# A planner's new numbers, filter-row DMAs behind the last root, and a last slab shared with GpSimd

## Chip, cores, metric

One core of one Trainium2 chip. The metric is the time of one execution in microseconds of device time (us). One core alone has no second die to compare with, so a run counts as slow when it is over 1.5% above the fastest of its kernel. Verdicts use fast runs alone and call 2% a difference; each kernel was timed in five rounds beside the kernel before on the same chip, and the ratios are read with their intervals.

## The reference

```python
def reference(A_x, A_w_r, A_w_i, B_x, B_w_gate, B_w_up, B_w_down):
    x  = A_x                                   # 1 x 2048 x 640, bf16
    xn = _layernorm(x)                         # over the 640 columns, eps 1e-5
    X  = rfft2(xn) * (A_w_r + 1j * A_w_i)      # spectral filter, 2048 x 321
    s  = irfft2(X)
    g  = silu((gelu(xn @ B_w_gate) * (xn @ B_w_up)) @ B_w_down)   # 640 -> 1536 -> 640
    return x + s * g
```

The kernel does both Fourier transforms by matmuls. The 2048 rows are 16 slabs of 128.

## The kernel before

Every instruction is a task with a cost. A planner in Python, run on the host while the program is built, simulates the engines and a model of the DMA bus, and the order in which it starts the tasks becomes the order of each engine's instructions. On the chip each engine runs its list in that order. So a number in the planner costs no instruction; it can only reorder them.

```python
    def ready(self, t, e, now):                     # earliest start of task t on engine e
        ...
        at = max([0.0] + [... a.done + (... self.MARGIN[e]
                 + ((1500 if a.size else 150) if e == "PE" and a.start > 20000 else 0)) for a in t.after])
        ...
        if t.size and e == "SP":                    # a DMA: not further ahead of the bus than BACKLOG = 3500 ns
            at = max(at, self.wire - self.BACKLOG)
    def run(self):
            ...
            if t.land:                              # the first loads: landing times typed in from a measurement
                self.wire = max(self.wire, t.land - 1000)
                t.done = t.land
            elif t.size:                            # every other DMA: the model of the bus
                self.wire = max(self.wire, now + occ + 900) + t.size * t.slow / 340.0
                t.done = self.wire + (... 2600 if now < 21000 else 1000) + t.lag
```

**Roots**: GpSimd computes 1/sqrt(variance) of each slab (L430, L431), and VectorE applies it (L445). **Fold**: four VectorE operations (L511, L514, L520, L525) fold two slabs for the first transform; TensorE multiplies (L538, L539), ScalarE copies the product out of PSUM into `mc` (L297; two buffers), and the sync queue stores it (`D<-mc`).

**Filter rows**: twelve small DMAs on GpSimd that put single rows of the filter in place. After them GpSimd loads slabs of x again for the residual (`xr`, 160 KB each, three buffers).

```python
            turned_w[0].append(add(lambda e, ...: nc.gpsimd.dma_start(out=D4[a:a + n, b, ri, 0:width], in_=rows(w, first, n, width)),
                                   "POOL", (600, 600), (9, ri, b, a), after=[roots[3]], size=5152))
```

## Time and profile before

| | before |
|---|---|
| time, median of 6 runs | 204.5 us (204.39 to 204.67) |
| span of the profiled run | 202.4 us, granted clock 0.996 |
| TensorE busy | 195.9 us, 97% |
| its only wait in mid-kernel | 0.5 us at 25 us (0.65 from start to start) |
| last matmul ends / last output issued | 197.86 / 199.47 us |

TensorE is busy from the first to the last microsecond of its list, so the time is the sum of its work, plus what it stops, plus the end after its last matmul. The lines are in the prediction. In the views, PE is TensorE, DVE VectorE, ACT ScalarE, POOL GpSimd, SP the sync queue; a timeline line has start, duration, engine, source line, operation, and in brackets how long the engine was idle before it and what ended that.

### The profile page before, as it was taken

The numbers are of one execution on the slowest core, as the hardware profiler recorded it, in microseconds if no ns is written. First come the engines' busy times: TensorE is split into PE (matmuls) and PEld (weight loads), VectorE is DVE, ScalarE is ACT, GpSimd is POOL, SyncE is SP. The second block draws the span as 40 slices with busy tenths as digits, with TensorE's granted clock in tenths as the row PEclk, the third lists the DMA queues.
The fourth block names the chain that finished last, engine by engine and source line by source line (L and its number), as shares of the span: only waits on it lengthen the run. The fifth ranks groups of instructions, "written<-read, shape, count | busy, mean of one in ns | idle before, by whom it ended". The sixth has DMA issues, their size and how long they took to land.

```text
span 202.4 us, 4147 instructions
## 1 busy us (share of the span) xinstructions
PE 195.9 (97%) x1546; PEld 118.2 (58%) x1546; DVE 147.9 (73%) x317; ACT 127.6 (63%) x227; POOL 33.4 (16%) x70
## 2 busy tenths in 40 slices
PE   7999999999999999999999999999999999999991
PEld 2994344677544555677754555567755554557780
DVE  3587889999422239899999898963226887778783
ACT  4989789975632566768776756533286656775521
POOL 2495454590000000000000000000000222111200
PEclk9999999999999999999999999999999999999998
DMA  6999999598859776313342111105900433344422
GB/s 175 327 320 340 352 390 221 122 171 292 272 176 371 221 198 130 102 59 89 117 130 74 60 65 65 68 0 156 416 14 0 120 88 102 108 110 130 133 97 66
DMA packets 35398, 32.62 MB, mean 161 GB/s; under 512 B 10798, under 2 KB 32306, under 8 KB 35378
## 3 DMA queue, kind: packets, MB, share of 16 engines
q1 hardware_dynamic: 33938, 29.49, 48.9%
q0 software_dynamic: 1152, 2.66, 5.1%
q10 hardware_dynamic: 288, 0.20, 0.6%
q8 instruction: 12, 0.20, 0.4%
q14 instruction: 8, 0.07, 0.1%
HBM read 22.51 MB, written 9.19 MB: 157 GB/s over the span
## 4 chain that ended last, share of the span: by engine, by line
PE 95%; DMA 1%; DVE 1%; issue 0%; ACT 0%; DVEq 0%
PE pg L891 26%; PE pu L891 25%; PE pg L968 13%; PE pu L968 13%; PE sp L703 3%; PE sp L836 3%; PE sp L778 2%; PE sp L812 2%; PE sp L538 2%; PE sp L676 2%; DMA X<-in_A_x_dram 1%; PE sp L696 1%; PE sp L830 1%; PE sp L461 1%; PE sp L484 1%; PE sp L659 0%
## 5 line engine op out<-in xcount | busy, mean ns | idle before, releaser
L891 PE MATMUL pg<-xnT,Wg 128*128 128x512 bf16 (+1 forms) x245 | 57.5, 366 | 0.0
L891 PE MATMUL pu<-xnT,Wu 128*128 128x512 bf16 (+1 forms) x245 | 57.5, 366 | 0.0
L908 DVE TENSOR_TENSOR uT<-pu,ge 128x512 bf16<-128x512 f32 x46 | 31.7, 689 | 25.3 <-PE pu L891 24.8
L904 ACT ACTIVATE ge<-pg 128x512 bf16<-128x512 f32 x46 | 27.7, 601 | 32.2 <-PE pg L891 32.1
L968 PEld LDWEIGHTS <-uT 128*128 128x128 bf16 x396 | 37.8, 98 | 13.6
L891 PEld LDWEIGHTS <-Wg 128*128 128x128 bf16 x285 | 25.4, 99 | 23.1
L891 PEld LDWEIGHTS <-Wu 128*128 128x128 bf16 x285 | 25.0, 98 | 21.2
L932 POOL DMA_DIRECT2D xr<-in_A_x_dram x16 | 8.9, 560 | 140.1 <-DVE res L956 140.1
L968 PE MATMUL pg<-Wd,uT 128*128 128x320 bf16 (+2 forms) x204 | 30.2, 293 | 0.0
L968 PE MATMUL pu<-Wd,uT 128*128 128x320 bf16 (+1 forms) x192 | 29.8, 297 | 0.0
L297 ACT CAST ma<-sp 128x644 bf16<-128x644 f32 (+1 forms) x32 | 23.4, 793 | 6.3 <-PE sp L703 3.3
L977 ACT ACTIVATE th<-pg 128x320 f32<-128x320 f32 (+2 forms) x17 | 7.3, 427 | 9.5 <-PE pg L968 8.7
L297 ACT CAST Vt<-sp 128x640 bf16<-128x640 f32 x16 | 10.8, 691 | 3.7 <-PE sp L812 3.7
L297 ACT CAST IU<-sp 128x640 bf16<-128x640 f32 x16 | 10.7, 693 | 3.0 <-PE sp L778 3.0
L982 DVE SCALAR_TENSOR_TENSOR G<-th,pu 128x320 bf16<-128x320 f32 (+1 forms) x16 | 7.7, 481 | 6.3 <-ACT th L977 6.2
L982 DVE SCALAR_TENSOR_TENSOR G<-th,pg 128x320 bf16<-128x320 f32 (+1 forms) x16 | 7.7, 479 | 6.2 <-ACT th L977 6.1
L977 ACT ACTIVATE th<-pu 128x320 f32<-128x320 f32 (+1 forms) x16 | 7.0, 440 | 7.4 <-PE pu L968 7.3
L297 ACT CAST mc<-sp 128x640 bf16<-128x640 f32 x16 | 10.8, 700 | 1.2 <-PE sp L539 1.2
L297 ACT CAST Z<-sp 128x1024 bf16<-128x1024 f32 x8 | 7.9, 1015 | 1.8 <-PE sp L676 1.7
L431 POOL TENSOR_TENSOR RSTD<-MVA,mh 128x1 f32<-128x1 f32 x12 | 8.1, 678 | 2.0 <-DVE MVA L413 1.2
L416 ACT ACTIVATE th<-X 128x640 bf16<-128x640 bf16 x11 | 8.1, 738 | 0.2
L756 DVE TENSOR_TENSOR R<-Y 64x644 bf16<-64x644 bf16 x16 | 7.8, 490 | 0.4
(109 smaller groups left out, 242.5 us busy)
## 6 DMA issues: line engine op xcount, KB each, us to landing
BU<-D SPq DMA_DIRECT2D x8, 640.0 KB
D<-mc SPq DMA_DIRECT2D x8, 320.0 KB
xr<-in_A_x_dram POOLq DMA_DIRECT2D x16, 160.0 KB, 3.5
D<-IU SPq DMA_DIRECT2D x8, 320.0 KB
out_dram<-res SPq DMA_DIRECT2D x15, 160.0 KB
Wg<-in_B_w_gate_dram SPq DMA_DIRECT2D x6, 320.0 KB
Wu<-in_B_w_up_dram SPq DMA_DIRECT2D x6, 320.0 KB
WF<-D SPq DMA_DIRECT2D x8, 161.0 KB
```

The lines of the kernel that those rows point to most:

```text
L297: return nc.scalar.copy(out=out, in_=in_) if e == "ACT" else nc.vector.tensor_copy(out=out, in_=in_)
L416: nc.scalar.activation(out=place(junk, (D,)), in_=x, func=ACT.Copy, scale=-1.0 / D, accum_out=less)
L431: nc.gpsimd.tensor_tensor(out=rstd, in0=var, in1=mh, op=ALU.pow)
L703: nc.tensor.matmul(into(q, ri), lhsT=sZ.tile[:, q, ri, :], rhs=FM[:, kinds[q][2] + (4 if ri and kind == 0 else 0), :], start=False, stop=T ...
L756: nc.vector.tensor_tensor(out=o, in0=Yf[:, ::-3, :], in1=Yf[:, 1:3, :], op=ALU.subtract)
L891: nc.tensor.matmul(ps.tile[:, lo:hi], lhsT=w[:, c, t * P:(t + 1) * P], rhs=XR[:, c, lo:hi] if early else xnT[:, c, grp * 512 + lo:grp * 51 ...
L904: nc.scalar.activation(out=ge.tile, in_=pg.tile if src is None else src, func=ACT.Gelu_apprx_tanh)
L908: nc.vector.tensor_tensor(out=u.tile, in0=pu.tile if src is None else src, in1=ge.tile, op=ALU.mult)
L932: nc.gpsimd.dma_start(out=sx.tile, in_=xv[:, n1, :])
L968: nc.tensor.matmul(ps.tile[:, 0:hi - lo], lhsT=uT[grp, ks[i]].tile[:, j * P:(j + 1) * P], rhs=Wd[:, ks[i], lo:hi], start=(i == 0), stop=(i ...
L977: nc.scalar.activation(out=th.tile[:, 0:hi - lo], in_=ps.tile[:, 0:hi - lo], func=ACT.Tanh, scale=0.5)
L982: nc.vector.scalar_tensor_tensor(out=G2.tile[:, lo:hi], in0=th.tile[:, 0:hi - lo], scalar=1.0, in1=ps.tile[:, 0:hi - lo], op0=ALU.add, op1 ...
```

## The change

The intent: take the filter-row DMAs out of GpSimd's way while it computes roots, take two operations out of VectorE's closing chain, and give the planner numbers that were thought to be nearer to the chip. One more warm-up matmul (dummy work at the start, `keep_warm`) comes with it. The diff is shortened; `...` marks cuts, and the comments are mine.

```diff
- ... (1500 if a.size else 150) if e == "PE" and a.start > 20000 ...
+ ... (1500 if a.size else 250) if e == "PE" and a.start > 20000 ...      # larger margin for TensorE
-                self.wire = max(self.wire, t.land - 1000)
+                self.wire = max(self.wire, t.land - 3200)                # the bus model
-    t = warmed = keep_warm(5, [t])
+    t = warmed = keep_warm(6, [t])
-            ss = [... (0, 4, k, t) if k else (1, -1, k, t) ...]           # rank of the column sums ...
+            ss = [... (0, 4, k, t) ...]
-            sums_out[k] = add(... (0, 9) ...)                             # ... and of their copy
+            sums_out[k] = add(... (0, -1) ...)
-                out=D4[...], in_=rows(...)), "POOL", (600, 600), ..., after=[roots[3]], size=5152))
+                out=D4[...], in_=rows(...)), "POOL", (600, 600), ..., after=[roots[15]], size=5152))
-  t = add(ends, "PE", c_pe(480, 320, 161, 161, 161, 161), ...)            # likewise 480 -> 530 in the inverse
+  t = add(ends, "PE", c_pe(550, 320, 161, 161, 161, 161), ...)            # dearer row-tile visits
-                nc.vector.tensor_tensor(out=yg...)                        # and res, in finish()
+                (nc.gpsimd if last and lo == 0 else nc.vector).tensor_tensor(out=yg...)
```

The larger bus number means: the planner takes the bus for free 3.2 us, not 1.0 us, before each typed-in landing time.

More of the change, by code (lines that the diff above doesn't have):

```diff
@@ L143, in ready @@
                 return None
-        at = max([0.0] + [a.start + a.engs[e][0] if a.on == e == "PE" else a.done + (0 if a.on == e and not a.size else self.MARGIN[e] + ((1500 if a.size else 150) if e == "PE" and a.start > 20000 else 0)) for a in t.after])
+        at = max([0.0] + [a.start + a.engs[e][0] if a.on == e == "PE" else a.done + (0 if a.on == e and not a.size else self.MARGIN[e] + ((1500 if a.size else 250) if e == "PE" and a.start > 20000 else 0)) for a in t.after])
         more = {}
@@ L472, in sums @@
                     nc.tensor.matmul(pt.tile[:, 1, 256 + t:257 + t], lhsT=w[:, c, t * P:t * P + P], rhs=ones, start=(c == 0), stop=(c == 4), skip_group_check=True)
-            ss = [add(lambda e, t=t: sums(e, t), "PE", (132, 370), (0, 4, k, t) if k else (1, -1, k, t), after=[got[t], raw[n1]], use=[pt]) for t in range(2)]
-            sums_out[k] = add(lambda e: copy_on(e, WSUM[:, 2 * k:2 * k + 2], pt.tile[:, 1, 256:258]), {"ACT": c_act(2), "DVE": c_dve(2, 1, True)}, None, (0, 9), after=ss, use=[pt])
+            ss = [add(lambda e, t=t: sums(e, t), "PE", (132, 370), (0, 4, k, t), after=[got[t], raw[n1]], use=[pt]) for t in range(2)]
+            sums_out[k] = add(lambda e: copy_on(e, WSUM[:, 2 * k:2 * k + 2], pt.tile[:, 1, 256:258]), {"ACT": c_act(2), "DVE": c_dve(2, 1, True)}, None, (0, -1), after=ss, use=[pt])
     for n1 in range(4):
@@ L610 @@
             turned_w[0].append(add(lambda e, ri=ri, w=w, a=a, n=n, b=b, first=first, width=width: nc.gpsimd.dma_start(
-                out=D4[a:a + n, b, ri, 0:width], in_=rows(w, first, n, width)), "POOL", (600, 600), (9, ri, b, a), after=[roots[3]], size=5152))
+                out=D4[a:a + n, b, ri, 0:width], in_=rows(w, first, n, width)), "POOL", (600, 600), (9, ri, b, a), after=[roots[15]], size=5152))
         turned_w[0].append(add(lambda e, ri=ri, w=w: nc.gpsimd.dma_start(out=D4[15:16, 1, ri, L:LP], in_=w[0:1, 0:1]), "POOL", (600, 600),
-                            (9, ri, 2), after=[roots[3]], size=64))
+                            (9, ri, 2), after=[roots[15]], size=64))
     def fetch(G):
@@ L713, in spectral @@
             if kind == 0:
-                t = add(ends, "PE", c_pe(480, 320, 161, 161, 161, 161), (0, 102 + 4 * G), new=[*pes, sE], use=[sz, sZ],
+                t = add(ends, "PE", c_pe(550, 320, 161, 161, 161, 161), (0, 102 + 4 * G), new=[*pes, sE], use=[sz, sZ],
                         after=[z_done, zt_done, tab_in["fm"], tab_in["ft"]])
@@ L842, in inverse @@
             if k == 0:
-                t = add(ends, "PE", c_pe(480, 320, 160, 160, 160, 160), (0, 299 + 4 * j), after=v_done + [tab_in["im"], tab_in["it"]],
+                t = add(ends, "PE", c_pe(530, 320, 160, 160, 160, 160), (0, 299 + 4 * j), after=v_done + [tab_in["im"], tab_in["it"]],
                         new=[*pys, y4], use=svs)
@@ L950, in f1 @@
                     place(yg, (D,))
-                nc.vector.tensor_tensor(out=yg.tile[:, lo:hi], in0=y.tile[:, n1 % 2, lo:hi], in1=G2.tile[:, lo:hi], op=ALU.mult)
+                (nc.gpsimd if last and lo == 0 else nc.vector).tensor_tensor(out=yg.tile[:, lo:hi], in0=y.tile[:, n1 % 2, lo:hi], in1=G2.tile[:, lo:hi], op=ALU.mult)
             def f2(e):
@@ L955, in f2 @@
                     place(res, (D,))
-                nc.vector.tensor_tensor(out=res.tile[:, lo:hi], in0=yg.tile[:, lo:hi], in1=sx.tile[:, lo:hi], op=ALU.add)
-            t = add(f1, "DVE", c_dve(hi - lo), rank, after=[y_done[n1]] + done, new=[yg] if first else [], use=[y, G2] if first else [y, G2, yg])
-            t = add(f2, "DVE", c_dve(hi - lo), rank, after=[t, xr], new=[res] if first else [], use=[yg, sx] if first else [yg, sx, res])
+                (nc.gpsimd if last and lo == 0 else nc.vector).tensor_tensor(out=res.tile[:, lo:hi], in0=yg.tile[:, lo:hi], in1=sx.tile[:, lo:hi], op=ALU.add)
+            slow = last and lo == 0
+            t = add(f1, *(("POOL", (700, 800)) if slow else ("DVE", c_dve(hi - lo))), rank, after=[y_done[n1]] + done, new=[yg] if first else [], use=[y, G2] if first else [y, G2, yg])
+            t = add(f2, *(("POOL", (700, 800)) if slow else ("DVE", c_dve(hi - lo))), rank, after=[t, xr], new=[res] if first else [], use=[yg, sx] if first else [yg, sx, res])
             dma(lambda: outv[:, n1, lo:hi], lambda: res.tile[:, lo:hi], (0, 0, n1), 256 * (hi - lo), after=[t], use=[res])
```

## The prediction

> **What bounds the kernel now.** I read the page first, then TensorE's waits, then the timeline where TensorE waited, then the timeline of the end. From the page, busy time and the chain that ended last:
>
> ```profile
> PE 195.9 (97%) x1546; PEld 118.2 (58%) x1546; DVE 147.9 (73%) x317; ACT 127.6 (63%) x227; POOL 33.4 (16%) x70
> ...
> PE 95%; DMA 1%; DVE 1%; issue 0%; ACT 0%; DVEq 0%
> ```
>
> TensorE is busy for 195.9 of 202.4 us and is 95% of the chain. Its waits, complete:
>
> ```profile
> PE sp L369 <- DVE uT L362: 1.2, 1, 1.2
> PE sp L538 <- DVE mb L525: 0.5, 1, 0.5
> PE sp L461 <- DMA X<-in_A_x_dram: 0.2, 1, 0.2
> ```
>
> Of the 6.5 us in which TensorE is not busy, 1.2 precede its first matmul, 0.5 are one wait in mid-kernel, 0.2 are for the first slab of x, and the remaining 4.5 are the stretch after its last matmul (197.03 + 0.83 = 197.86 us, to the end at 202.4). Busy is not full rate, so I checked it: the chain shows five 512-column matmuls of L891 in 1.08 us over and over, that is 216 ns each. Nothing in the middle can be sped up by reordering.
>
> The one wait in mid-kernel, from the timeline around it (start, duration, engine, line, idle before):
>
> ```profile
> 18.30 0.52 POOL L610 DMA_DIRECT2D D<-in_A_w_i_dram  x1 [0.71 <-DMA D<-in_A_w_r_dram]
> 18.90 0.18 POOL L430 TENSOR_SCALAR MVA<-MVA 128x1 f32<-128x1 f32 x1
> 19.16 0.57 POOL L431 TENSOR_TENSOR RSTD<-MVA,mh 128x1 f32<-128x1 f32 x1
> 19.69 0.61 POOL L610 DMA_DIRECT2D D<-in_A_w_i_dram  x1
> 20.33 0.58 POOL L431 TENSOR_TENSOR RSTD<-MVA,mh 128x1 f32<-128x1 f32 x1
> 20.94 0.45 DVE L445 TENSOR_SCALAR s<-X,MVA,RSTD 128x640 bf16<-128x640 bf16 x1 [1.86 <-POOL RSTD L431]
> 24.85 0.48 DVE L525 TENSOR_TENSOR mb<-ma 128x640 bf16<-128x640 bf16 x1
> 25.39 0.39 PE L538 MATMUL sp<-mb,F1T 128*128 128x512 bf16 x1 [0.49 <-DVE mb L525]
> ```
>
> This is a chain through GpSimd. Vector had the variance of slab 4 ready at 17.47 + 0.15 = 17.62 us (L413 in the timeline). Its root on GpSimd started at 20.33, 2.7 us late, because GpSimd was issuing filter-row DMAs and waiting for earlier ones to land. Vector stood idle for 1.86 us, so the fold of slabs 4 and 5 ended at 25.33 and TensorE waited for it.
>
> The end, after TensorE's last matmul:
>
> ```profile
> 198.21 0.29 DVE L986 TENSOR_TENSOR mc<-s,pg 128x128 f32<-128x128 bf16 x1
> 198.42 0.28 DVE L956 TENSOR_TENSOR res<-yg,xr 128x256 bf16<-128x256 bf16 x1
> 198.62 0.28 DVE L951 TENSOR_TENSOR yg<-s,G 128x256 bf16<-128x256 bf16 x1
> 198.73 0.94 SPq L304 DMA_DIRECT2D out_dram<-res  x2
> 198.82 0.28 DVE L989 SCALAR_TENSOR_TENSOR yg<-th,mc 128x128 bf16<-128x128 f32 x1
> 199.02 0.28 DVE L956 TENSOR_TENSOR res<-yg,xr 128x256 bf16<-128x256 bf16 x1
> 199.22 0.21 DVE L996 TENSOR_TENSOR res<-yg,xr 128x128 bf16<-128x128 bf16 x1
> 199.47 0.35 ACTq L998 DMA_DIRECT2D out_dram<-res  x1
> ```
>
> Here Vector is the bound: one small operation every 0.20 us. The last output is issued by 199.82 and the span ends 2.6 us later.
>
> **What the Trainium skill says.** "TensorE: Matmul & The Clock Gate", Part 1, gives start-to-start 426.7 ns cold and 215.7 ns warm for 512 columns. The trace agrees: 216 ns warm, and the weight loads of the warm-up matmuls stand 0.42 us apart (1.62, 2.04, 2.47 us in the timeline). "GPSIMD Engine Reference", section 3.1, puts two-input elementwise work at about 2.6 cycles of 1.2 GHz per element, and section 1 says that GpSimd shares its SBUF interfaces with VectorE, with contention from Vector instructions that have two SBUF inputs. The trace of before has no wide two-input operation on GpSimd, but it shows the contention: L430 on 128x1 takes 0.19 us at 33.11, and 1.57 us at 38.99, under a row of two-input Vector operations. "DMA: Bandwidth & Descriptors", on SWDGE (Anatomy of one DMA), gives a fixed cost near 2 us; here the twelve filter-row DMAs need 5.2 to 6.3 us from issue to landing, the xr loads 3.5 us, so the measured values are used.
>
> **The change part by part.** The diff touches four things, and the built order of instructions shows what becomes of them.
>
> 1. Filter-row DMAs after the last root. All twelve now stand behind the last root on GpSimd. The root of slab 4 can start at about 17.7 instead of 20.33. Vector's apply (L445) no longer waits 1.86 us, so the fold should end about 2 us earlier, near 23.4. TensorE meets that fold later in its own order: one more L891 group of five (1.08 us) precedes it. Reach in the new kernel without stalls: 25.39 - 0.49 - 0.17 (an uncertain part of the same pause: start-to-start it cost 0.66 beyond the matmul) + 1.08 = about 25.8, over 2 us after the fold. The pause goes. Gain 0.5 to 0.65 us, all on the path, since TensorE has no idle time after it.
>
> The DMAs themselves move to about 43 us (last root before: 42.97 + 0.55). Twelve issues of about 0.56 us are 6.7 us, plus about 2 us of waits for the queue's earlier landings (2.0 us before): issued by about 52, landed by about 58 at 6 us each. The first reader is the load of the filter tile at 63.41. Margin 5 us; cost 0. The xr loads behind them are needed from 158 us on.
>
> 2. The new numbers for the planner. The same matmuls are planned; counted by kind, the two orders differ by one warm-up matmul and nothing else. The row-tile groups (L696, L830: 16 visits) stay 16, each still costing about 0.1 us on entry and on leaving; calling them dearer changes only the order. Gain 0 directly.
>
> 3. Sixth warm-up matmul. It costs 0.43 us cold. The five end near 3.34 and the first slab of x is there at 3.71, so it fills the 0.18 us and overruns to 1.21 + 6 x 0.427 = 3.77: 0.06 late. The second slab lands for 5.33 after two more cold matmuls, which absorbs that. Cost 0 to 0.06. The ten one-column sum matmuls (L472) now precede the first ten L891 matmuls. These run cold until 6.25 us (0.11 instead of 0.056 us), so up to 4 x 0.055 = 0.2 us may be saved; but the roots of slabs 1 to 3 now come in another order, and the apply of slab 3 may be met early. I count 0.
>
> 4. GpSimd finishes columns 0 to 255 of the last slab. Vector loses two operations of 0.28 us; one (L956 at 198.42) is in the closing chain, so the last Vector operation comes 0.20 us earlier. Against it: 256 x 2.6 / 1.2 = 0.55 us (estimate by the skill's page) plus a fixed part of 0.2 (from L430's 0.19) to 0.5 is 0.75 to 1.05 us for each of two. They start near 196.8, where a 640-wide two-input Vector operation (0.48 us) is in the way, and the second meets the closing chain of two-input operations from 198.4 on. So GpSimd ends between 198.5 and 199.5. In the sync queue its output stands ahead of Vector's, which was ready for issue near 199.3 before. If GpSimd ends after about 198.9 it starts to delay both. Net: -0.2 to +0.4, counted as 0.
>
> Sum: -0.6 (part 1) + 0 + 0 + 0 = 204.49 - 0.6 = 203.9 us.
>
> **The rivals.**
> - New waits replace the old one. The whole order after 6 us is reshuffled, some 300 groups on TensorE, and an in-order engine stalls where the plan was too hopeful. For: the fold of slabs 6 and 7 now has two more Vector operations (L511, L908: about 1.0 us) ahead of its L525, which started at 39.03 before; it is met at about 40.95. Against: Vector gains the 1.9 us, so it should be done by 39.5; and the planner's margin for TensorE's waits grew by 0.1 us. Later, Vector is 95% busy from 80 to 120 us; the first spectral result R ended near 85.1 and TensorE used it at 86.4 before, and the new order leaves about the same. Two or three waits of 0.2 to 0.4 us would give 204.4 to 204.8.
> - GpSimd becomes the end of the kernel, as in part 4: 204.2 to 204.6.
> - The filter tile comes late, because the DMAs on GpSimd crawl under Vector's load. Then the sync queue stands behind one wait and everything for the spectral stage shifts: 206 or more. The 5 us of margin speak against it.
> - All goes well: the pause gone, 0.2 from the cold start, 0.2 at the end: 203.4.
>
> **Range and chances.** Three runs lie within 0.11 us, so noise is small. The gain is capped by what TensorE idles: even everything together is about 1 us (0.5%). Losses are limited only by new stalls. Predicted 203.9, range 203.2 to 204.7. Faster by over 2% would need 4.1 us out of the 6.5 idle ones: 1%. Slower by over 2% needs the late filter tile: 2%. Within 2%: 97%.
>
> **What would show it.** Right: no wait of TensorE for mb L525; GpSimd's root for slab 4 near 17.7 us and Vector's L445 without the 1.86 us; TensorE's last matmul ending near 197.3; the filter DMAs issued from 43 to 52 us, and the filter tile's load no later than before (63.41). Wrong: new lines among TensorE's waits; a gap at the filter load; GpSimd's two operations ending after 199 us with the sync queue waiting for GpSimd at the end.

## More of the kernel before

**RB**: the first two gate and up tiles are multiplied from raw x, before its statistics are known, and repaired on VectorE by a row tile that a DMA (`RB<-D`, after `D<-th`) spreads over the partitions:

```python
            m = add(... nc.vector.scalar_tensor_tensor(in0=RB[:, 1], ...), "DVE", ..., after=[out, rb_in, sums_out[k]])   # L921
            normed.append(add(... nc.vector.tensor_tensor(in1=RB[:, 0], op=ALU.mult), "DVE", ..., after=[m]))            # L923
```

## The result and the profile after

| | before | after |
|---|---|---|
| time, median of 6 runs | 204.5 us | 204.59 us (204.35 to 205.19) |
| TensorE busy | 195.9 us | 195.7 us |
| pause of TensorE at 25 us | 0.65 us | none |
| stops of TensorE from 26 to 55 us, start to start | none | 0.20 + 0.18 + 0.41 us |
| last matmul ends | 197.86 us | 198.00 us |
| from there to the issue of the last output | 1.61 us | 1.41 us |

The ratio of after to before is 1.0009, 95% interval 0.9994 to 1.0025. Ratios here are the mean time of one kernel's fast runs over that of the other's of the same rounds, so not quite the ratio of the medians. So the gain of 0.6 us that I predicted was not there, although the time lies in my range.

TensorE's waits after (us in total, times, longest):

```profile
PE sp L369 <- DVE uT L362: 1.2, 1, 1.2
PE sp L461 <- DMA X<-in_A_x_dram: 0.5, 1, 0.5
PE pu L891 <- DMA Wu<-in_B_w_up_dram: 0.3, 1, 0.3
PE sp L538 <- ACT mc L297: 0.2, 1, 0.2
```

The wait for `mb L525` is gone, as predicted; a small new one, for a copy by ScalarE, stands in its place. The view of waits shows less than is lost: a stop costs TensorE more from start to start than the idle that the view counts.

The timeline after, from the moved root to the new stops:

```profile
17.47 0.55 POOL L431 TENSOR_TENSOR RSTD<-MVA,mh 128x1 f32<-128x1 f32 x1 [0.68 <-DVE MVA L413]
...
23.46 0.48 DVE L525 TENSOR_TENSOR mb<-ma 128x640 bf16<-128x640 bf16 x1
...
28.89 0.69 ACT L297 CAST mc<-sp 128x640 bf16<-128x640 f32 x1 [1.85 <-DMA D<-mc]
...
30.09 0.75 DVE L921 SCALAR_TENSOR_TENSOR IU<-RB,WSUM,IU 128x512 f32<-128x512 f32 x1 [1.68 <-DMA RB<-D]
...
37.09 0.97 PE L969 MATMUL pu<-Wd,uT 128*128 128x320 bf16 x6
...
43.92 0.38 PE L538 MATMUL sp<-mb,F1T 128*128 128x512 bf16 x1 [0.24 <-ACT mc L297]
```

The first two lines are what I promised: the root starts when the variance is there, and the fold ends at 23.94 us instead of 25.33. The next two are new. ScalarE waits 1.85 us for a buffer whose store has not landed, and VectorE 1.68 us for the row tile RB. Before, neither waited; this is the first L921 in the timeline of before:

```profile
31.58 0.74 DVE L921 SCALAR_TENSOR_TENSOR IU<-RB,WSUM,IU 128x512 f32<-128x512 f32 x1
```

Then come the stops.

The page agrees: part 4 of the page (the chain that ended last) was 95% TensorE and 1% DMA before, and is now

```profile
PE 79%; DMA 10%; DVE 5%; SPq 2%; issue 1%; ACT 1%; DVEq 0%; ACTq 0%
```

and the chain in order of time has as its longest piece of that stretch

```profile
22.70 7.37 DMA RB<-D
```

Start and duration: the row tile left the queue at 22.70 us and landed at 30.07. I had the planner print its own dates while the program was built (arithmetic on the host, not a time of the chip): it expected RB at 30.20 us in the kernel before and at 28.18 us in the changed one. The chip did not follow the new number.

The end went as hoped. From the timeline after:

```profile
196.98 0.85 POOL L951 TENSOR_TENSOR yg<-s,G 128x256 bf16<-128x256 bf16 x1 [4.34 <-DVE G L983]
...
197.91 0.67 POOL L956 TENSOR_TENSOR res<-yg,xr 128x256 bf16<-128x256 bf16 x1
...
199.41 0.35 ACTq L999 DMA_DIRECT2D out_dram<-res  x1
```

GpSimd is done at 198.58 us, before VectorE, and the last output follows the last matmul 0.20 us sooner. So the trace has -0.65 (pause), +0.79 (new stops), -0.20 (end); the start came out even. The sum is -0.06 us, next to the measured 0.0 of the two spans.

### The profile page after: what moved, and what is told of

It reads as the page before. It is cut to its first block, busy times and chain, and to the rows that moved or that the text cites. A ratio compares the mean times of both kernels' runs of the same rounds, so it can differ in the third digit from the quotient of the medians.

```text
span 202.4 us, 4151 instructions
## 1 busy us (share of the span) xinstructions
PE 195.7 (97%) x1547; PEld 117.8 (58%) x1547; DVE 146.8 (73%) x314; ACT 127.2 (63%) x228; POOL 32.0 (16%) x72
## 4 chain that ended last, share of the span: by engine, by line
PE 79%; DMA 10%; DVE 5%; SPq 2%; issue 1%; ACT 1%; DVEq 0%; ACTq 0%
PE pu L891 20%; PE pg L891 20%; PE pg L969 11%; PE pu L969 11%; DMA RB<-D 4%; DMA D<-th 3%; PE sp L703 3%; PE sp L836 3%; DMA Wu<-in_B_w_up_dram 2%; PE sp L778 2%; PE sp L812 2%; PE sp L676 2%; SPq L502 1%; DMA D<-in_A_w_r_dram 1%; PE sp L696 1%; PE sp L830 1%
## 5 line engine op out<-in xcount | busy, mean ns | idle before, releaser
L969 PEld LDWEIGHTS <-uT 128*128 128x128 bf16 x396 | 37.7, 98 | 14.2 <-DVE uT L908 0.3
L891 PEld LDWEIGHTS <-Wg 128*128 128x128 bf16 x285 | 25.2, 98 | 23.4
L969 PE MATMUL pg<-Wd,uT 128*128 128x320 bf16 (+2 forms) x204 | 30.5, 293 | 0.0
L969 PE MATMUL pu<-Wd,uT 128*128 128x320 bf16 (+1 forms) x192 | 29.5, 297 | 0.0
L297 ACT CAST ma<-sp 128x644 bf16<-128x644 f32 (+1 forms) x32 | 23.4, 793 | 7.4 <-PE sp L703 3.4
L756 DVE TENSOR_TENSOR R<-Y 64x644 bf16<-64x644 bf16 x16 | 7.8, 490 | 0.4
L758 DVE TENSOR_TENSOR R<-Y 64x644 bf16<-64x644 bf16 x16 | 7.8, 486 | 0.3
```

The source lines that it names most:

```text
L297: return nc.scalar.copy(out=out, in_=in_) if e == "ACT" else nc.vector.tensor_copy(out=out, in_=in_)
L756: nc.vector.tensor_tensor(out=o, in0=Yf[:, ::-3, :], in1=Yf[:, 1:3, :], op=ALU.subtract)
L758: nc.vector.tensor_tensor(out=o, in0=Y[:, 0], in1=Y[:, 1], op=ALU.add)
L891: nc.tensor.matmul(ps.tile[:, lo:hi], lhsT=w[:, c, t * P:(t + 1) * P], rhs=XR[:, c, lo:hi] if early else xnT[:, c, grp * 512 + lo:grp * 51 ...
L969: nc.tensor.matmul(ps.tile[:, 0:hi - lo], lhsT=uT[grp, ks[i]].tile[:, j * P:(j + 1) * P], rhs=Wd[:, ks[i], lo:hi], start=(i == 0), stop=(i ...
```

## The experiments

All kernels gave correct results. "Frozen" means that the planned order of a kernel is kept and single tasks are moved in it; otherwise the planner ran again. The runs of before are from the same chip and rounds: one set of eleven for e1 to e4, one for e5 to e8, one for e9 to e12. The traces are of one execution per kernel and not always of a typical one: e8's was its slowest run (206.02 us), e5's its second slowest (204.41), e9's its fastest (204.33).

| run | what it is | median, us | before, us | ratio, 95% interval |
|---|---|---|---|---|
| e1 | before, frozen; rows moved | 204.53 | 204.46 | 0.9996 [0.9974, 1.0019] |
| e2 | before, frozen; tail on GpSimd | 204.21 | 204.46 | 0.9982 [0.9965, 0.9999] |
| e3 | both | 203.63 | 204.46 | 0.9951 [0.993, 0.9973] |
| e4 | after with the old bus model | 203.43 | 204.46 | 0.9947 [0.9928, 0.9965] |
| e5 | e1 with the rows behind three xr loads | 203.92 | 204.65 | 0.9977 [0.9958, 0.9996] |
| e6 | after, frozen; VectorE's order mended | 204.56 | 204.65 | 1.0003 [0.999, 1.0017] |
| e7 | after, planner told RB's landing | 204.89 | 204.65 | 1.0027 [1.0007, 1.0047] |
| e8 | before with the new bus model only | 205.23 | 204.65 | 1.0034 [1.0014, 1.0055] |
| e9 | after, frozen; store ahead of Wd | 204.84 | 204.61 | 1.0005 [0.9981, 1.003] |
| e10 | e9 and e6 together | 204.54 | 204.61 | 0.9988 [0.9963, 1.0012] |
| e11 | e4, frozen; Wd ahead of the store | 205.25 | 204.61 | 1.0029 [1.0006, 1.0052] |
| e12 | e5 and e2 together | 203.82 | 204.61 | 0.9957 [0.9934, 0.998] |

### The parts that move work

e1 keeps before's plan and moves the twelve row tasks behind the last root when the tasks are emitted:

```diff
-        for t in plan.run():
-            t.emit(t.on)
+        order = plan.run()
+        rows_t = [t for t in order if t in turned_w[0] and t.on == "POOL"]
+        order = [t for t in order if t not in rows_t]
+        at = order.index(roots[15]) + 1
+        for t in order[:at] + rows_t + order[at:]:
+            t.emit(t.on)
```

> The order of before is kept instruction for instruction on TensorE, Vector, Scalar and the sync queue; only the twelve filter-row DMAs move behind the last root on GpSimd. Theory A (the pause of 0.65 us at 25 us is real time, and the changed kernel lost it again through its new order): TensorE's wait for mb L525 is gone, the last matmul ends near 197.2 instead of 197.87, time 0.6 us below before (about 203.9, ratio 0.997). Rival B (TensorE's slack at that point is fictitious: a later wait, such as the one for the Scalar copy of mc, catches what is gained whatever the order): another wait of 0.4 to 0.7 us appears between 25 and 60 us and the time is that of before within 0.2 us.

e2 puts only the last slab's two operations on GpSimd (the `nc.gpsimd if last and lo == 0` lines of the diff); e3 is e1 and e2 together.

> The order of before; only the multiply and the add of columns 0 to 255 of the last slab go to GpSimd. Theory A: GpSimd needs 0.85 + 0.67 us as in the changed kernel and ends before Vector; the last issue of an output comes 0.20 us earlier after the last matmul, time 0.2 us below before (ratio 0.999). Rival C (the end is set by the landing of the outputs in the sync queue, not by Vector's last operation): same time within 0.05 us although Vector ends 0.2 us earlier.

> Both parts in the order of before, with none of the planner's new numbers. Theory A: the gains add up to 0.8 us, time about 203.7 (ratio 0.996), faster than both kernels. Rival B: 0.2 us at most.

e2 came out 0.25 us under its before, median to median, and in its trace 1.40 us lie between the last matmul and the last output, as in the changed kernel. The tail is worth what its chain of small operations says. In e1 the pause at 25 us is gone from the trace and yet the time is the same; the wait that took it back is not where rival B looked for it (25 to 60 us) but at 93 us. TensorE's waits, and two timelines, of e1:

```profile
PE sp L778 <- DVE R L756: 1.1, 1, 1.1
```

```profile
56.35 1.29 ACT L297 CAST mc<-sp 128x640 bf16<-128x640 f32 x2 [3.54 <-DMA D<-mc]
...
88.83 0.83 DVE L735 TENSOR_TENSOR mc<-WF,mb 128x1288 bf16<-128x1288 bf16 x1 [2.15 <-DMA WF<-D]
```

The second fence follows one delay through 35 us. ScalarE waits 3.5 us for a store before it can make its last two copies; only behind their stores may the sync queue read the whole first transform back (the regroup, L583), which goes out at 60.86 us instead of 57.35; every filter load behind it is late; VectorE waits for one at 88.83; TensorE stops for 1.1 us at 93. Why was the store late? The moved rows push GpSimd's three 160 KB residual loads from 43.5 to 49.1 us, among the stores and table loads. Or the rows' own small packets are in the way. e5 was to tell them apart: same as e1, but the rows go behind those three loads (`order[:at] + xr_t + rows_t + ...`, with `xr_t` the first three).

> The kernel before in its own planned order, the twelve filter-row DMAs moved behind GpSimd's last root AND behind its first three residual loads (xr), so that those loads keep their old place at about 43.5 us. Theory D: in e1 the moved rows pushed the three 160 KB residual loads from 43.5 to 49.1 us, onto the table loads and the stores of the first transform; a store landed late, ScalarE's copy waited 3.5 us for its buffer, and the regroup on the sync queue went out at 60.9 instead of 57.4 us, which made the third filter tile late (Vector 2.1 us, TensorE 1.1 us near 93 us). With the loads back in place: regroup issued before 59 us, no TensorE wait at L778, pause at 25 us still gone, 203.9 us (203.6 to 204.1), 0.5 below before. Rival E: the rows' own small packets slow the stores: regroup again near 61 us, TensorE wait of about 1 us at L778, 204.5 us.

In e5 the loads leave at 42.90 us, the regroup at 58.85, TensorE's waits have none after its start, and the time is 203.92 us, as the theory of the displaced loads (D) said. The interval of e5's ratio lies below 1; e1's does not. But this does not settle it. The two intervals overlap, and e1's runs spread more (203.67 to 205.24 us). e3 has rows and loads where e1 has them, and its five fast runs (203.63 us; its profiled run was slow, 207.37 us, so its trace is not used) are as quick as e12's, with the loads back in place (ratios 0.9951 and 0.9957). In e4 the loads leave as late as in e1 (49.31 us), and the regroup goes out at 58.70. In e2 the loads are in their old place (43.62 us), and yet ScalarE waits 2.19 us for a store and the regroup goes out at 59.80. So the chain above is what one execution of e1 lost; that the place of the loads causes it, and what it costs on average, is not shown.

e12 adds e2's tail to e5:

> The kernel before in its own planned order with e5's place for the filter rows (behind the three residual loads) and the tail's two operations on GpSimd; no planner number changed. If the parts add (e5 0.73 below its before, e2 0.25 below its): 203.6 us (203.4 to 203.8), ratio to before about 0.9955, pause at 25 us gone, last output issued 0.2 us sooner after the last matmul. Rival M: the rows and the tail share GpSimd and do not add: 203.9 us as e5 alone.

203.82 us, just above the range that I wrote; the ratio, 0.9957, is what I wrote. The parts add within their intervals. So the moved work is worth 0.8 to 1.0 us, more than my prediction gave it. The changed kernel has it, and something takes it back.

### The part that only reorders

e4 is the changed kernel with one number put back:

```diff
-                self.wire = max(self.wire, t.land - 3200)
+                self.wire = max(self.wire, t.land - 1000)
```

> The changed kernel with the bus model of before (land - 1000 instead of land - 3200) and everything else new. With it Vector's first L921, which needs the broadcast RB, stands five places later in Vector's order, behind the fold of slabs 6 and 7. Theory A (the new bus model puts L921 too early, Vector stands 1.68 us for RB, and uT L908 and the fold come late): that wait of Vector shrinks to under 0.5 us, TensorE's two stops for uT L908 (0.20 + 0.17 us near 37 and 39 us) go, time 0.4 to 0.8 us below the changed kernel: 203.7 to 204.2. Rival D (the margins or the new start order are to blame): the time stays at 204.4 to 204.7.

e8 is the converse, the kernel before with that number alone changed to 3200:

> The kernel before with nothing but the new bus model (its planner then dates RB at 28.33 us instead of 30.20). Theory F: Vector waits 1 to 2 us for RB near 28 to 30 us, the pause at 25 us (0.65) stays, new stops of 0.3 to 0.8 us follow: 204.8 to 205.3 us. Rival I: the new model only hurts together with the other numbers of the change: 204.5 us as before, within 0.2.

e4 is 203.43 us, below the range that I wrote and the fastest kernel, 1.0 us under its before, and its trace has no wait of TensorE after the start. e8 is slower than before by 0.6 us between the medians and 0.7 by the ratio (1.0034), with all three new things: VectorE waits 1.0 us for RB, ScalarE 1.76 us for a store, TensorE stops for 1.56 us in all between 26 and 55 us. From the timelines of its ScalarE and VectorE:

```profile
29.51 0.69 ACT L297 CAST mc<-sp 128x640 bf16<-128x640 f32 x1 [1.76 <-DMA D<-mc]
...
30.72 0.75 DVE L921 SCALAR_TENSOR_TENSOR IU<-RB,WSUM,IU 128x512 f32<-128x512 f32 x1 [1.02 <-DMA RB<-D]
```

**So the new bus model costs about as much as the rest of the change gains.** The rest of the planner's numbers, the sixth warm-up and the sums gain nothing that can be seen: e4 has them and e3 has not, and their ratios are 0.9947 and 0.9951.

How does a model of the bus lose time? Two differences between e4 and the changed kernel stand out. The sync queue's timeline, first the changed kernel's, then e4's:

```profile
18.35 1.01 SPq L304 DMA_DIRECT2D Wd<-in_B_w_down_dram  x1
19.46 2.92 SPq L304 DMA_DIRECT2D D<-mc  x1
22.70 0.34 SPq L304 DMA_DIRECT2D RB<-D  x1
```

```profile
18.52 0.93 SPq L304 DMA_DIRECT2D D<-mc  x1
19.50 0.43 SPq L304 DMA_DIRECT2D Wd<-in_B_w_down_dram  x1
20.03 3.00 SPq L304 DMA_DIRECT2D RB<-D  x1
```

With the new model the bus looks free, so the planner sends the 1.25 MB load of Wd ahead of the first transform store. With the old one it holds Wd back and the store goes first. All kernels planned with the new model and read here (after, e6, e7, e8) have Wd first. The other difference is VectorE's order: in the changed kernel L921 stands ahead of the fold of slabs 6 and 7, because RB was dated 28.18.

The windows view (busy time in the stretch, in order PE, PEld, DVE, ACT, POOL) shows what both do to the helpers; before, after, e4:

```profile
20.00:30.00 10.00, 9.51 (x46) 4.23 (x45) 8.48 (x22) 8.08 (x19) 5.25 (x11) 1.00 1.07 369
```

```profile
20.00:30.00 10.00, 10.00 (x49) 4.62 (x48) 6.96 (x16) 7.22 (x17) 2.37 (x6) 1.00 1.08 366
```

```profile
20.00:30.00 10.00, 9.95 (x49) 4.61 (x48) 8.46 (x20) 9.99 (x24) 3.12 (x8) 1.00 1.07 367
```

From 30 to 40 us both helpers are full in these three kernels (9.8 to 10.0 of 10 us each), so what they idle before that is not made up until TensorE feels it. Here is the idle time of VectorE and ScalarE together from 20 to 40 us, against TensorE's stops from 26 to 55 us. (Stops are start-to-start excess over 0.12 us. Steps of 0.22 us in traces with 16 to 18 fewer matmul records are lost records and left out.)

| kernel | idle of the two, us | stops of TensorE, us |
|---|---|---|
| e4 | 1.76 | 0 |
| e12, e5, e1 | 2.57, 2.61, 2.70 | 0.19, 0.28, 0 |
| before, e2 | 3.51, 3.75 | 0, 0 |
| e6 | 4.59 | 0.48 |
| after | 5.92 | 0.79 |
| e8 | 5.99 | 1.56 |
| e11 | 6.38 | 1.13 |
| e9, e7 | 6.94, 6.98 | 1.31, 1.65 |

Up to 3.75 us of idle time TensorE has no stop over 0.28 us; from 4.6 us on it stops for 0.48 us or more. This is a pattern over twelve traces and not yet a cause. I then tried to undo the two waits one at a time.

**e6**: the changed kernel, frozen, with the fold of slabs 6 and 7 moved into VectorE's idle time and one use of RB moved behind a product that TensorE waits for.

```diff
+        order = [t for t in order if t not in fold_t[3]]
+        at = min(order.index(t) for t in rb_t)
+        order = order[:at] + fold_t[3] + order[at:]          # and: the last L921 behind the next L908
```

> The changed kernel in its own planned order, with two moves on VectorE only: the four fold operations of slabs 6 and 7 (1.6 us together) go ahead of the first use of the row tile RB, where Vector sat idle 1.68 us, and the last first-step use of RB goes behind the next gate product. Theory F: the new stops of TensorE at 37.1, 39.3 and 43.9 us (0.20, 0.17, 0.42 us) come from Vector being late after it waited for RB; filled, they go: 203.8 us (203.6 to 204.1), no TensorE wait after 10 us. Rival G: the stops come from elsewhere (ScalarE's own order, the DMA stores): 204.5 us as the changed kernel, stops still there.

A miss: 204.56 us. VectorE's wait and the stop at 43.9 us are gone, but the one near 39.8 us grew to 0.48. ScalarE still waited 1.75 us for the store.

**e7**: the changed kernel planned again, the planner told that RB lands later (`rb_in.lag = 1900`).

> The changed kernel with its new bus model, only the planner is told that this one load RB lands 1.9 us later than its bus model says (the planner then has 30.1 us; with the new model alone it has 28.18, the chip landed it at 30.0). Theory F: this one date is what the new bus model costs: Vector's wait for RB under 0.3 us, no stop of TensorE over 0.2 us between 30 and 50 us, 203.4 to 203.9 us, near e4. Rival H: the new bus model costs by other dates too (stores, regroup): 204.3 us or more.

A miss, and in the wrong direction: 204.89 us. VectorE no longer waits for RB. The chain of e7 has another transfer in its place:

```profile
19.67 9.36 DMA D<-mc
29.11 0.12 ACT mc L297
```

That is the store behind Wd: 9.36 us from issue to landing. (The planner's arithmetic dates this store's landing in the changed kernel at 26.64 us; there ScalarE could start on its buffer only at 28.89. So this date is over 2 us early too.) Then come ScalarE's copy, the statistics behind it, a root on GpSimd, and VectorE, which waits 2.18 us for that root. Theory F (RB alone) fell here, and J (the store) was formed.

**e9** puts the store ahead of Wd in the changed kernel, **e10** does that and e6's moves, and **e11** is the converse on e4:

```diff
+        big = min(wd_t, key=order.index)                     # the 1.25 MB load of Wd
+        order.remove(big)
+        order.insert(order.index(stored[0]) + 1, big)        # e9, e10; e11 inserts it at index(stored[0]) instead
```

> The changed kernel in its own planned order with one swap on the sync queue: the first transform store (D<-mc, 320 KB) goes out ahead of the 1.25 MB load of Wd instead of behind it, as in before and in e4. Theory J, formed after e6 and e7: all kernels planned with the new bus model (the changed one, e6, e7, e8) issue Wd first; the store then lands late, ScalarE waits 1.75 to 2.15 us near 28 to 31 us for its buffer (0 in before, e4, e5), and that is the larger half of the 1.1 us. Expected: ScalarE's wait gone, Vector's wait for RB (1.7 us) still there, the stop at 43.9 us gone, those at 37 to 39 us halved: 204.1 us (203.9 to 204.3). Rival K: ScalarE's wait costs nothing, its work is caught up: 204.5 us or more.

> e9's swap on the sync queue and e6's two moves on VectorE together, nothing else. Theory J: both engines are then free of their waits between 25 and 31 us and the stops of 0.79 us between 37 and 44 us are gone: 203.6 us (203.3 to 203.9), near e4 (203.43), no wait of TensorE after 10 us above 0.2. Rival L: another date of the new bus model costs it, the stops come back elsewhere: 204.3 us or more.

> The converse on the fastest kernel so far: e4 (the changed kernel with the old bus model, 203.43 us) in its own planned order with one swap, Wd's 1.25 MB load ahead of the first transform store, as the new bus model had it. Theory J: the store lands late again, ScalarE waits 1 to 2 us for its buffer before 31 us, and TensorE stops for 0.3 to 0.8 us before 50 us: 203.8 to 204.3 us. Rival K: the order on the queue is harmless: 203.4 us, within 0.15 of e4.

e11 hit harder than J said. With one swap on the queue the fastest kernel (203.43 us, ratio 0.9947) becomes the slowest of the twelve (205.25, ratio 1.0029; on another chip, but each stands against its own before). Its chain, in order of time:

```profile
19.79 9.42 DMA D<-mc
```

ScalarE then waits 2.64 us, VectorE 2.85 us for ScalarE, and TensorE stops at 30.5 and 32.1 us. So the order Wd, then store, is enough to lose time. How much of e11's loss is the swap's? The same TensorE group, with the same work before it, starts at these times in e4 and in e11:

```profile
9.27 0.72 PE L891 MATMUL pg<-XR,Wg 128*128 128x128 bf16 x10
```

```profile
10.02 0.72 PE L893 MATMUL pg<-XR,Wg 128*128 128x128 bf16 x10
```

The swapped DMA is issued at 18.66 us. e11's last matmul ends 1.90 us after e4's: 0.75 us of that is older than the swap, and 1.13 us are the stops behind it. Over the traces of the table this group starts between 9.16 us (e7) and 10.02; 0.33 us of e4's lead over before, and 0.34 of its lead over the changed kernel, are already there at that point. Whether such a difference at the start belongs to a kernel or to one execution is not shown.

The swap is not all of the loss: e9 missed, 204.84 us. There ScalarE's wait for the store is gone, but the stop near 44 us, which J said would go, stayed (0.41 us), and from the timelines of its ScalarE and VectorE

```profile
32.34 0.63 ACT L906 ACTIVATE ge<-IU 128x512 bf16<-128x512 f32 x1 [2.06 <-DVE IU L925]
```

```profile
30.30 0.75 DVE L923 SCALAR_TENSOR_TENSOR IU<-RB,WSUM,IU 128x512 f32<-128x512 f32 x1 [2.12 <-DMA RB<-D]
```

the wait moved: VectorE waits 2.12 us for RB (line numbers are shifted by two here), and ScalarE 2.06 us for VectorE's repaired tile, since ScalarE's list too was written for RB at 28.18. e10 missed as well, 204.54 us; its profiled run was slow (209.65 us, clock 0.947), so I can't say what stopped its fast runs.

What is shown: the new bus model is the part that costs (e4, e8); the queue order it makes costs by itself (e11); moving work away from RB's wait, the store's wait, or both, in the changed kernel's own order brings back at most 0.2 us when the medians are taken against their own before (e6, e9, e10; by e10's ratio it is 0.4, but one of its runs of before took 206.03 us), while planning again with the old model brings back all. What is only argued: that the lists of all three, sync queue, VectorE and ScalarE, are laid around the two wrong dates and have to change together. The test that is missing is the changed planner told both dates at once, RB's and the store's.

## Why the prediction was right or wrong

The time fell in the range and in the right class, within 2%. That was luck rather than the working: the range of 1.5 us also held "no change", the time lies 0.11 us under its upper edge, and the gain that I forecast did not come. The center was 0.7 us too low, and the step that failed is a term that I set to zero (2 below). Three of my own signs say so: a new line among TensorE's waits, the last matmul ending at 198.00 us instead of near 197.3, and the filter tile's load leaving at 67.43 us instead of no later than 63.41.

1. **Rows behind the last root, gain 0.5 to 0.65 us.** The mechanism was right: root at 17.47 (said 17.7), fold ended at 23.94 (said near 23.4), pause gone, TensorE at the fold at 25.82 (said 25.8). e5 puts the gain at 0.5 (ratio) to 0.7 us (medians), e3 against e2 at 0.6. "Cost 0" for the rows themselves was not checked far enough: I looked at the rows' own reader and its 5 us of margin, not at the loads behind them in the same queue. One execution of e1 lost the whole gain with these loads late; e3, with the same places, did not lose it. In the changed kernel the loads also leave late (50.4 us) and the regroup too (60.97), but VectorE shows no wait for a filter tile there.
2. **Planner's numbers: "calling them dearer changes only the order. Gain 0 directly."** The first half is true and the second does not follow. That step weighs only the dearer row-tile visits and not the bus number at all. This is the step that failed: one of the numbers costs 0.7 us alone (e8) and takes about 1.2 us from the changed kernel (1.0009 against e4's 0.9947). I counted matmuls in the two orders and found them equal. I did not look at the sync queue's order, where Wd had moved ahead of a store, nor ask at what time the planner believed RB to land and compare it with the trace.
3. **Sixth warm-up and sums, counted 0.** Right as far as the traces show: TensorE starts its first up tile at 6.83 us after and 6.84 before. The 0.2 us saved cold went into a wait of 0.3 us for Wu.
4. **GpSimd's share of the end, -0.2 to +0.4, counted 0.** The favourable end came true: -0.20 us in the traces, -0.25 in e2. GpSimd's operations took 0.85 and 0.67 us (I said 0.75 to 1.05 for each; the second came in below).

The rival "new waits replace the old one" named the right kind of loss (204.4 to 204.8 us) and came close to the place, the fold of slabs 6 and 7. I argued it away with "Vector gains the 1.9 us, so it should be done by 39.5"; its L525 ran at 40.72, after VectorE had stood 1.68 us for RB. TensorE met that fold at 41.34 us without a stop; its stops were at 37.09 and 39.30 (matmuls with Wd, L969) and at 43.92 (ScalarE's copy).

With the measured sizes the sum reads 204.5 - 0.65 (pause) - 0.20 (end) + 0.79 (stops) = 204.4, where 204.59 was measured.

## What to carry to other kernels

When a planner's model of transfers is changed, compare its landing dates with a trace before the kernel is timed: here a model with two dates 2 us early cost about as much as two real improvements gained. After a planner change read the order of the DMA queue first, above all a large load that has passed a small store whose buffer someone waits for. And when work is moved to the back of a queue, ask what stood behind it.

## What the Trainium skill lacked or had wrong

- "GPSIMD Engine Reference", section 3.1 (about 2.6 cycles an element for two inputs; by that 0.55 us is an estimate for 256): the two operations took 0.85 us, beside a two-input VectorE operation, and 0.67 us. The 0.30 and 0.12 us more have no figure there: the section names a dispatch part for GpSimd without a number. Whether they are that part or contention is not separated here.
- "DMA: Bandwidth & Descriptors", Anatomy of one DMA (a fixed cost near 2 us): the same twelve row DMAs took 5.2 to 6.3 us to land at 11 to 21 us of the kernel before, 1.8 to 2.7 us at 44 to 50 us of the changed one, and 2.8 to 6.5 us in e1. A nearly constant cost does not describe these; what sets the difference no run here separates.
- The same page, Queues, rings and completion order, says that each DMA engine consumes descriptors in ring order. The runs fit that and add the size: a 320 KB store issued behind a 1.25 MB load took 9.36 and 9.42 us to land (e7, e11). Issuing it held the sync queue for 2.9 to 3.0 us, where other early stores took 0.3 to 1.0; in e4, where the load of RB comes next behind Wd, issuing that load took 3.00. No page that I read has that cost.
